# Attention with memory slots and a routed expert layer: queries loaded with the halves of a head's values on different partitions

## The chip, the cores and the metric

The kernel runs on one core of a Trainium2 chip. The core has a matrix engine (TensorE, "PE" in the profile), a vector engine (VectorE, "DVE"), an engine for activations (ScalarE, "ACT"), a general one (GpSimd, "POOL"), a sequencer that only issues transfers here (SyncE, "SP"), and 16 DMA engines. Data lie on 128 partitions in on-chip memory (SBUF); products of TensorE land in eight banks of PSUM. The metric is the time of one execution on the device in microseconds (us), as the median of several runs. Less is better.

## The reference

The first half is an attention with 32 memory slots, for 8 batches of 8 heads with 576 tokens of 64 values each. The second half routes each token (512 values, all its heads) to one of 8 experts, a two-layer network.

```python
a = softmax(phi)                       # over the 576 tokens, per slot
k_m = einsum('bhsm,bhsd->bhmd', a, k)  # 32 x 64 per head
v_m = einsum('bhsm,bhsd->bhmd', a, v)
scores = q @ k_m.T / 8                 # 576 x 32 per head
attn = softmax(scores)                 # over the 32 slots
x = attn @ v_m                         # 576 x 64 per head
logits = x @ w_gate + modality_bias[modality_id]
e = argmax(logits); gate = softmax(logits)[e]
out = gate * (relu(x @ w1[e]) @ w2[e])
```

Everything is float32.

## The kernel before, in words

The kernel finds out from the modality biases which expert the tokens will choose, loads that expert's two matrices once, and works on the assumption that all tokens go there; at the end it checks this, and would run a general path otherwise (it does not with these inputs).

**A batch has a memory step, a scores step and an expert step.** P = 128 partitions, HG = 4 heads (index j) by NG = 2 groups (index g) make the 8 heads. QP = 64 partitions hold a group's tokens, QC = 9 tokens on each. BL = 32 is the block that DVE's transpose turns by itself: a 32x32 block at a time, with no exchange between groups of 32 partitions. RA = 4 and RB = 5 columns of tokens make the two parts of a batch.

The memory step: the largest phi of each slot is found on DVE (`mem_max` and what follows), the exponentials are taken (`mem_exp`), their sums over a partition's nine tokens are made on POOL (`mem_sums`, lines 279 to 283). `kv_products` (line 388) multiplies them with keys and values on TensorE, in tiles of 64 rows by 32 columns, and then adds up the sums over partitions in eight small products (line 396). `kv_divide` divides: DVE makes the reciprocals (lines 472, 474), ACT scales (lines 482, 484). The keys are written twice each there, because the queries lie so that a head's 64 values are in two blocks of 32 on the *same* partitions, and need the keys of each half on every 32 partitions. `mem_turn` then turns keys and values with TensorE (line 146: two turns for the halves of the keys, one for the values), and ACT copies them from PSUM to SBUF (lines 514, 522).

The scores step: the queries, loaded by one DMA per batch (`load_queries`, line 180), are turned in place by DVE in four pieces, one for each j (`q_turn`, line 552). `scores` (line 564) multiplies them on TensorE with the keys in tiles of 32 rows by 32 columns: for each half u, each j, each g and each half a of a group's tokens one product, and the two halves u are added up in PSUM. `soften` and `normalise` make the softmax on DVE and ACT, and turn the weights so that slots lie on partitions (lines 591 to 623); `a_split` makes two parts of them, of which the expert products take one after the other (lines 657, 660).

The expert step: instead of multiplying the weights with the values and that with the first matrix, the kernel multiplies values and matrix first (`value_products`, line 730, in 64x32 tiles). `hidden` (line 776) then makes a piece of the hidden layer from the weights, ACT and DVE take the positive part in two parts (lines 789, 793), and `outputs` (line 812) multiplies with the second matrix. Each product of float32 values is made as three products of rounded parts. ACT scales a finished tile by the gate into one of two buffers `ob` (line 825), and SP stores it (lines 833, 837).

**What sets the order.** The instructions of each engine are written out in one order by a planner (`weave`): two lists, one of attention steps with due times and one of expert steps, are merged with the help of a table of durations (`TAKES`), rules for when a step's inputs are ready, and due times (`AHEAD`, `SPREAD`). No scheduler moves anything afterwards. Each engine goes through its list in order and waits where an input is not there yet. SP has one list as well: loads of keys, values, phi and queries, the stores of the outputs, and copies of the weights to DRAM. A DMA of SP waits for its buffer to be free, and all that stands behind it on SP waits too.

The queries of batch b + 2 are asked for right after the scores of batch b, whose buffer (`q_sb[b % 2]`) they take. Those of batch 1 come at the end of the first loads (`more_keys(0)`).

Of the kernel before, what the change touches and what calls it, by code (L numbers as in the profile page):

```python
# [54 lines left out]
def attn_moe(ctx: ExitStack, tc: tile.TileContext, q, k, v, phi, mod_id, w_gate, mod_bias, w1, w2, out):  # L55
# [23 lines left out]
    BUSY = 90, 10  # L79
# [23 lines left out]
    places = const.tile([P, 2], F32, name="places")  # L103
    busy = const.tile([P, 512], BF16, name="busy")
# [4 lines left out]
    kTs = [const.tile([P, 2, P], F32, name=f"kT{i}") for i in range(2)]  # L109
    vT = [const.tile([P, HG, M], F32, name=f"vT{b}") for b in range(B)]  # L110
# [31 lines left out]
    live = {}  # L142
# [35 lines left out]
    def load_queries(b, c0=0, n=QC):  # L178
        cols = slice(c0 * D, (c0 + n) * D)
        nc.sync.dma_start(q_sb[b % 2][:, :, cols], halves(q, b)[:, :, cols])  # L180
# [196 lines left out]
    def kv_products(b):  # L377
# [4 lines left out]
        live["psum"] = pk[:, :, 2 * D]  # L382
# [10 lines left out]
        for j in range(HG):  # L393
            for g in range(NG):
                half = slice(QP * g, QP * (g + 1))
                nc.tensor.matmul(
                    pk[M * j:M * (j + 1), g, 2 * D:2 * D + 1], lhsT=sums[half, j], rhs=ones_c[half],
                    start=True, stop=True, tile_position=(QP * g, M * j),
                )
# [30 lines left out]
    def first_divide():  # L430
# [11 lines left out]
        live["keys", 0] = wk.tile([P, 2, NG, 2, BL], F32, name="keys", bufs=2)  # L442
        live["values", 0] = wk.tile([P, NG, D], F32, name="values", bufs=2)
# [26 lines left out]
    def kv_divide(b):  # L470
# [5 lines left out]
        live["keys", b] = wk.tile([P, 2, NG, 2, BL], F32, name="keys", bufs=2)  # L476
        live["values", b] = wk.tile([P, NG, D], F32, name="values", bufs=2)
        for t in range(2):
            for g in range(NG):
                src = live["kvp"][:, g, t]  # L480
                if t:
                    nc.scalar.activation(live["values", b][:, g], src, AF.Copy, scale=rec[:, g])
                else:
                    nc.scalar.activation(
                        live["keys", b][:, :, g],
                        src.rearrange("p (u o d) -> p u o d", u=2, o=1).broadcast_to([P, 2, 2, BL]),
                        AF.Copy, scale=rec[:, g],
                    )
# [857 lines left out]
```

## Time and profile before

| what | before |
|---|---|
| median of 3 runs | 392.82 us (392.59 to 393.16) |
| the profiled execution | 392.55 us, its span 390.8 us |
| PE busy | 379.2 us, 97% of the span |
| DVE, ACT, POOL busy | 243.7, 144.8, 45.7 us |
| granted TensorE clock | 0.998 |
| scores, batches 1 to 7 (line 564, 32x288) | 448 records, 11.2 us of overlapping durations |
| key and value products (line 388) | 1008 records of 271 ns |
| sums (line 396) | 112 records of 167 ns |
| turns of keys and values (line 146), batches 1 to 7 | 14 and 7 records of about 272 ns |
| load of a batch's queries | 1152 KB, 7.8 us from issue to landing (median of 7) |
| DMA | 56.91 MB in 28700 packets |

The span runs from the first to the last instruction; the rest of an execution's time lies around it. A row of the chain or of a timeline has the start, the duration, the engine and the line, the tiles written and read, and how many instructions it stands for. Matmuls overlap: each has a duration of its own, and several run at once, so that what a group costs is read from starts and not from the sum of durations. A product of two float32 operands appears as two records. The mark [0.31 <-POOL sums] at a row's end says that the engine was idle that long before it and what ended the wait.

### The profile page before, as it was taken

How to read it: one execution, taken by the hardware profiler on the slowest of the kernel's cores; microseconds unless marked ns; L12 is line 12 of the kernel's file. 1: busy time of each engine (PE TensorE's matmuls, PEld its weight loads, DVE VectorE, ACT ScalarE, POOL GpSimd, SP SyncE). 2: the span in 40 equal slices, each digit the busy share in tenths (PEclk: the TensorE clock that was granted, in tenths of full speed). 3: DMA queues.
4: the chain of work that ended last, by engine and by line, in shares of the span. 5: the costliest groups of instructions: out<-in, count | busy, mean ns of one | idle time of the engine just before them, and what ended most of it. 6: DMA issues, size and time to landing. Idle time of an engine off the chain costs nothing.

```text
span 390.8 us, 10131 instructions
## 1 busy us (share of the span) xinstructions
PE 379.2 (97%) x4218; PEld 305.1 (78%) x4220; DVE 243.7 (62%) x613; ACT 144.8 (37%) x348; POOL 45.7 (12%) x112
## 2 busy tenths in 40 slices
PE   7899999999999999999999999999999999999993
PEld 3577885889679787887879887797868879698982
DVE  4787756895789377844786466864787558660400
ACT  2382434426234243433433334324432425250410
POOL 3247020023000300030000300003000200000000
PEclk9999999999999999999999999999999999999999
DMA  8999349435920672529111291514411011431112
GB/s 294 352 378 375 78 117 381 140 147 129 332 64 27 197 285 108 189 66 375 41 27 55 71 393 73 216 27 142 159 27 29 28 30 29 167 130 29 30 28 61
DMA packets 28700, 56.91 MB, mean 146 GB/s; under 512 B 3044, under 2 KB 8164, under 8 KB 28644
## 3 DMA queue, kind: packets, MB, share of 16 engines
q1 hardware_dynamic: 28368, 55.87, 42.6%
q8 instruction: 35, 0.57, 0.6%
q10 hardware_dynamic: 276, 0.30, 0.2%
q14 instruction: 21, 0.17, 0.1%
HBM read 37.28 MB, written 18.87 MB: 144 GB/s over the span
## 4 chain that ended last, share of the span: by engine, by line
PE 86%; DVE 5%; DMA 3%; ACT 2%; POOL 1%; issue 1%; SPq 0%; ACTq 0%; POOLq 0%
PE pe L812 48%; PE pe L776 26%; PE pe L730 3%; PE pair L564 3%; PE pair L388 3%; DMA q_sb<-in_q_dram 3%; PE pair L677 1%; PE pair L146 1%; DVE a L597 1%; ACT ob L825 1%; DVE a L591 0%; DVE mx L595 0%; PE pair L541 0%; POOL t2sums L279 0%; ACT exp L356 0%
## 5 line engine op out<-in xcount | busy, mean ns | idle before, releaser
L812 PE MATMUL pe<-w2h,hh 128*128 128x512 f32 x288 | 116.5, 405 | 0.0
L812 PE MATMUL pe<-w2h,hl 128*128 128x512 f32 x288 | 112.6, 391 | 0.0
L812 PE MATMUL pe<-w2l,hh 128*128 128x512 f32 x288 | 110.3, 391 | 0.0
L793 DVE SCALAR_TENSOR_TENSOR hl<-pe,hh 128x256 fp32r<-128x256 f32 (+2 forms) x158 | 57.9, 392 | 41.9 <-ACT hh L789 41.1
L812 PEld LDWEIGHTS pe<-w2h,hh 128*128 128x128 f32 x288 | 54.1, 188 | 21.2 <-issue 11.0
L789 ACT ACTIVATE hh<-pe 128x256 fp32r<-128x256 f32 (+2 forms) x158 | 53.3, 362 | 39.1 <-PE pe L776 38.7
L812 PEld LDWEIGHTS pe<-w2l,hh 128*128 128x128 f32 x288 | 54.0, 188 | 11.8
L812 PEld LDWEIGHTS pe<-w2h,hl 128*128 128x128 f32 x288 | 54.2, 188 | 9.6
L825 ACT ACTIVATE ob<-pe,gates 128x512 f32<-128x512 f32 x36 | 24.7, 689 | 77.5 <-issue 43.5
L776 PE MATMUL pe<-xbh,vwh 128*128 128x320 f32 x128 | 40.2, 314 | 0.1
L776 PE MATMUL pe<-xbh,vwl 128*128 128x320 f32 x128 | 39.5, 309 | 0.0
L776 PE MATMUL pe<-xbl,vwh 128*128 128x320 f32 x128 | 39.5, 309 | 0.0
L776 PE MATMUL pe<-xah,vwh 128*128 128x256 f32 x124 | 35.2, 286 | 0.6 <-ACT xah L657 0.4
L776 PE MATMUL pe<-xal,vwh 128*128 128x256 f32 x124 | 35.0, 284 | 0.3 <-DVE xal L660 0.3
L776 PE MATMUL pe<-xah,vwl 128*128 128x256 f32 x124 | 34.9, 283 | 0.0
L322 POOL COPY ts<-tm 32x4 f32<-32x4 f32 x24 | 4.8, 199 | 200.4 <-DVE tm L314 199.7
L776 PEld LDWEIGHTS pe<-xah,vwh 128*128 128x128 f32 x124 | 23.6, 191 | 3.1 <-ACT xah L646 1.6
L776 PEld LDWEIGHTS pe<-xbh,vwh 128*128 128x128 f32 x128 | 24.0, 188 | 1.2 <-issue 0.5
L776 PEld LDWEIGHTS pe<-xbl,vwh 128*128 128x128 f32 x128 | 24.0, 188 | 0.3
L776 PEld LDWEIGHTS pe<-xal,vwh 128*128 128x128 f32 x124 | 23.7, 191 | 0.8 <-DVE xal L660 0.5
L152 DVE TENSOR_TENSOR vwl<-pe,vwh 128x512 fp32r<-128x512 f32 x26 | 16.6, 678 | 12.0 <-ACT vwh L151 12.0
L776 PEld LDWEIGHTS pe<-xbh,vwl 128*128 128x128 f32 x128 | 24.0, 188 | 0.0
(171 smaller groups left out, 448.9 us busy)
## 6 DMA issues: line engine op xcount, KB each, us to landing
kv_sb<-in_k_dram SPq DMA_DIRECT2D x8, 1152.0 KB, 5.9
kv_sb<-in_v_dram SPq DMA_DIRECT2D x8, 1152.0 KB, 9.4
out_dram<-ob SPq DMA_DIRECT2D x64, 128.0 KB, 2.4
q_sb<-in_q_dram SPq DMA_DIRECT2D x7, 1152.0 KB, 7.8
ph<-in_phi_dram SPq DMA_DIRECT2D x7, 576.0 KB, 4.1
raw<-in_moe_w_dram SPq DMA_DIRECT2D x2, 1024.0 KB, 7.5
raw<-in_moe_w_dram SPq DMA_DIRECT2D x1, 1280.0 KB, 10.6
out_dram<-ob SPq DMA_DIRECT2D x4, 256.0 KB, 2.4
```

Of the source, the lines that this page charges most:

```text
L146: nc.tensor.transpose(dst, src, ident[:rows, :rows])
L152: nc.vector.tensor_tensor(l, src, h.bitcast(F32), op=ALU.subtract)
L322: nc.gpsimd.tensor_copy(ts_[BL * a:BL * (a + 1)], live["tm"][BL * o:BL * (o + 1)])
L388: nc.tensor.matmul(live["kvp"][M * j:M * (j + 1), g], lhsT=pe[half, j, c * M:(c + 1) * M], rhs=kv_sb[half, :, j, c * D:(c + 1) * D], start ...
L564: nc.tensor.matmul(sc[g][M * j:M * (j + 1), a, c0 * BL:(c0 + n) * BL].rearrange("p (c t) -> p c t", t=BL), lhsT=kTs[b % 2][p0:p0 + BL, u, ...
L597: nc.vector.tensor_tensor(x, x, m.broadcast_to(list(x.shape)), op=ALU.subtract)
L730: nc.tensor.matmul(pvs[g][M * j:M * (j + 1), :], lhsT=vT[b][rows, j, :], rhs=raw1[rows, j, cols], start=True, stop=not more, tile_position ...
L776: nc.tensor.matmul(ph[:, 0:n], lhsT=(vl if k == 2 else vh)[:, g, cols], rhs=xl if k == 1 else xh, start=(g == k == 0), stop=(g == NG - 1 a ...
L789: nc.scalar.activation(hs[0][:, f, h0:h0 + p1 - p0], live["ph", f][:, p0:p1], AF.Relu)
L793: nc.vector.scalar_tensor_tensor(hl, live["ph", f][:, p0:p1], 0.0, hh.bitcast(F32), op0=ALU.max, op1=ALU.subtract)
L812: nc.tensor.matmul(po, lhsT=tile_columns(hl if n == 1 else hh, f, t), rhs=(w2l if n == 2 else w2h)[:, f, :], start=(f == n == 0), stop=(f ...
L825: nc.scalar.activation(ob, po, AF.Copy, scale=gate_of(b, t))
```

## The change

From batch 1 on, queries are loaded in another layout. A token's 64 values are cut in halves u, and the halves go to different groups of 32 partitions: partition 64 g + 32 u + t holds, for each j, the half u of tokens 18 t to 18 t + 17. After DVE's turn (as before) the 64 values of a head lie on 64 partitions, and one token column is one moving column. So `scores` makes one product for each a, j and g, with 64 rows, and nothing is added up in PSUM. Batch 0 keeps the old layout (`first_scores`, `first_keys`).

- The load of a batch becomes 16 DMAs, one for each g, u and j, of 32 partitions with 18 runs of 128 bytes each. They are put in a list (`later`), and `load_some` issues one at each call of `hidden` or `outputs`. Batch 1's 16 are issued at once.
- Keys are not doubled any more: keys and values are divided together into one tile `kvn` (two ACT instructions instead of four), turned with two turns instead of three, and copied to `kvT` by one ACT copy instead of two.
- The sums over partitions are one product of 128 rows, 128 columns and two moving columns (`sides`, ones on the half of the partitions that belongs to g) instead of eight of one column.
- Since a group's tokens now lie as 2 t + a instead of 32 a + t, `normalise` writes the turned weights to every second column.
- The planner's table and rules get new numbers: `kv`, `kvT` and `s` shorter, the step after the sums at 1.2 instead of 1.8 before their end, batch 3's due times 4.0 later. Two more small products are made at the start to keep TensorE busy.

```diff
+    sides = const.tile([P, NG], F32, name="sides")
...
-    kTs = [const.tile([P, 2, P], F32, name=f"kT{i}") for i in range(2)]
-    vT = [const.tile([P, HG, M], F32, name=f"vT{b}") for b in range(B)]
+    kT0 = const.tile([P, 2, P], F32, name="kT0")
+    kvT = [const.tile([P, 1 + (b > 0), P], F32, name=f"kvT{b}") for b in range(B)]
+    vT = [x[:, int(b > 0)].rearrange("p (j m) -> p j m", j=HG) for b, x in enumerate(kvT)]
...
     def load_queries(b, c0=0, n=QC):
-        cols = slice(c0 * D, (c0 + n) * D)
-        nc.sync.dma_start(q_sb[b % 2][:, :, cols], halves(q, b)[:, :, cols])
+        if b == 0:
+            cols = slice(c0 * D, (c0 + n) * D)
+            nc.sync.dma_start(q_sb[b % 2][:, :, cols], halves(q, b)[:, :, cols])
+            return
+        src = q[b].rearrange("(j g) (t x) (u d) -> g u j t x d", g=NG, t=BL, u=2)
+        for g in range(NG):
+            for u in range(2):
+                p0 = QP * g + BL * u
+                to = q_sb[b % 2][p0:p0 + BL].rearrange("t j (x d) -> t j x d", d=BL)
+                for j in range(HG):
+                    later.append((to[:, j], src[g, u, j]))
+
+    def load_some(n=1):
+        for _ in range(min(n, len(later))):
+            nc.sync.dma_start(*later.pop(0))
...
-        for j in range(HG):
-            for g in range(NG):
-                half = slice(QP * g, QP * (g + 1))
-                nc.tensor.matmul(
-                    pk[M * j:M * (j + 1), g, 2 * D:2 * D + 1], lhsT=sums[half, j], rhs=ones_c[half],
-                    start=True, stop=True, tile_position=(QP * g, M * j),
-                )
+        nc.tensor.matmul(live["psum"], lhsT=sums.rearrange("p j m -> p (j m)"), rhs=sides, start=True, stop=True)
...
+        live["kv", b] = wk.tile([P, 2, NG, D], F32, name="kvn", bufs=2)
+        for g in range(NG):
+            nc.scalar.activation(live["kv", b][:, :, g], live["kvp"][:, g], AF.Copy, scale=rec[:, g])
...
             load_queries(1)
+            load_some(16)
...
+    def mem_turn(b):
+
+        to = pair_of_banks(1)[:, 0, 0:2 * P]
+        for t in range(2):
+            turn(to[:, t * P:(t + 1) * P], live["kv", b][:, t].rearrange("p g d -> p (g d)"))
+        nc.scalar.copy(kvT[b].rearrange("p t s -> p (t s)"), to)
...
+    def scores(b):
         sc = [pair_of_banks(g) for g in range(NG)]
+        qT = q_sb[b % 2].rearrange("p j (a x) -> p j a x", a=2)
+        for a in range(2):
+            for j in range(HG):
+                for g in range(NG):
+                    rows = slice(QP * g, QP * (g + 1))
+                    nc.tensor.matmul(
+                        sc[g][M * j:M * (j + 1), a, 0:QC * BL], lhsT=kvT[b][rows, 0, M * j:M * (j + 1)],
+                        rhs=qT[rows, j, a], start=True, stop=True, tile_position=(QP * g, M * j),
+                    )
...
-                nc.vector.transpose(aT[:, g].rearrange("p (c a t) -> p a c t", a=2, t=BL), a[:, g])
+                nc.vector.transpose(aT[:, g].rearrange("p (c t a) -> p a c t" if b else "p (c a t) -> p a c t", a=2, t=BL), a[:, g])
...
     def hidden(i, part, f, terms=range(3), groups=range(NG), to=None, evict=True):
 
 
+        load_some()
...
     def outputs(t, fs, finish, terms=range(3)):
 
 
+        load_some()
...
-    AHEAD, SPREAD = (5.8, 5.0), 0.55
+    AHEAD, EARLIER, SPREAD = (5.8, 5.0), {3: -4.0}, 0.55
...
-            t = max([0.0] + [done[n] + (0.1 if n[0] != "sums" else -1.8) for n in s[0][2] if n[0] != "g"])
+            t = max([0.0] + [done[n] + (0.1 if n[0] != "sums" else -1.2) for n in s[0][2] if n[0] != "g"])
```

The order of instructions at three places, before and then with the change. First PE from the sums of batch 1 to its scores (L388 key and value products, L396 sums, L812 expert products, L146 turns, L564 scores; with the change L403, L408, L816, L148, L548).

```order
L388 MATMUL pair_941<-kv_sb,exp 32x128 x72
L396 MATMUL pair_941<-ones_c,sums 32x1 x8
...
L812 MATMUL pe<-w2h,hh 128x512
L812 MATMUL pe<-w2h,hl 128x512
L812 MATMUL pe<-w2l,hh 128x512
L146 MATMUL pair_1051<-ident,keys 128x128 x2
L146 MATMUL pair_1051<-ident,values 128x128
L812 MATMUL pe<-w2h,hh 128x512
L812 MATMUL pe<-w2h,hl 128x512
L812 MATMUL pe<-w2l,hh 128x512
L564 MATMUL pair_1060<-q_sb_102,kT_79 32x288 x2
```

```order
L403 MATMUL pair_980<-kv_sb,exp 32x128 x72
L408 MATMUL pair_980<-sides,sums 128x2
...
L816 MATMUL pe<-w2h,hh 128x512
L816 MATMUL pe<-w2h,hl 128x512
L816 MATMUL pe<-w2l,hh 128x512
L148 MATMUL pair_1077<-ident,kvn 128x128 x2
L816 MATMUL pe<-w2h,hh 128x512
L816 MATMUL pe<-w2h,hl 128x512
L816 MATMUL pe<-w2l,hh 128x512
L548 MATMUL pair_1084<-q_sb_102,kvT_81 32x288
```

Nine expert products stood between sums and turns, now six; batch 2 alone keeps the twelve shorter ones that it had. The scores are 16 rows of one product each, where they were 16 rows of two.

Second, PE at batch 6: the key and value products inside the expert products of one output tile (pe_3602, with the change pe_3573; each group of three rows is one step of that tile).

```order
L812 MATMUL pe_3602<-w2h_107,hh_113 128x512
L812 MATMUL pe_3602<-w2h_107,hl_114 128x512
L812 MATMUL pe_3602<-w2l_108,hh_113 128x512
L388 MATMUL pair1_3615<-kv_sb_103,exp_3581 32x128 x72
L396 MATMUL pair1_3615<-ones_c_73,sums_3589 32x1 x8
L812 MATMUL pe_3602<-w2h_107,hh_113 128x512
```

```order
L816 MATMUL pe_3573<-w2h_107,hh_113 128x512
L816 MATMUL pe_3573<-w2h_107,hl_114 128x512
L816 MATMUL pe_3573<-w2l_108,hh_113 128x512
L403 MATMUL pair1_3589<-kv_sb_103,exp_3552 32x128 x72
L408 MATMUL pair1_3589<-sides_75,sums_3560 128x2
L816 MATMUL pe_3573<-w2h_107,hh_113 128x512
```

Before, four groups of three expert products of that tile come ahead of L388; now five do, so the products start three expert products later in the tile. Batch 2's stand where they stood.

Third, SP from the loads of batch 1's keys on (L176 keys and values, L180 queries, L837 output stores, L173 phi; with the change L178, L195, L841, L175).

```order
L176 DMA kv_sb<-in_k_dram 128x4x576
L176 DMA kv_sb<-in_v_dram 128x4x576
L180 DMA q_sb_102<-in_q_dram 128x4x576
L180 DMA q_sb_101<-in_q_dram 128x4x576
L837 DMA out_dram<-ob 64x512 x4
L173 DMA ph_104<-in_phi_dram 128x4x288
L173 DMA ph_105<-in_phi_dram 128x4x288
```

```order
L178 DMA kv_sb<-in_k_dram 128x4x576
L178 DMA kv_sb<-in_v_dram 128x4x576
L195 DMA q_sb_102<-in_q_dram 32x18x32 x16
L195 DMA q_sb_101<-in_q_dram 32x18x32 x16
L841 DMA out_dram<-ob 64x512 x4
L175 DMA ph_104<-in_phi_dram 128x4x288
L175 DMA ph_105<-in_phi_dram 128x4x288
```

Where one DMA stood for batch 1 and one for batch 2, 16 stand each, ahead of the first four output stores. Later batches' 16 are spread over the following stores and copies in groups of 2 to 13.

More of the change, by code (lines that the diff above doesn't have):

```diff
@@ L78, in attn_moe @@
     EPS = 1e-9
-    BUSY = 90, 10
+    BUSY = 92, 10
     FAR = float(1 << 20)
@@ L141, in attn_moe @@
     stage_pool = stage_ctx.enter_context(tc.tile_pool(name="stage", bufs=1, side="right"))
-    live = {}
+    live, later = {}, []
     def turn(dst, src, rows=P):
@@ L441, in first_divide @@
         live["recs"] = recs
-        live["keys", 0] = wk.tile([P, 2, NG, 2, BL], F32, name="keys", bufs=2)
-        live["values", 0] = wk.tile([P, NG, D], F32, name="values", bufs=2)
+        live["keys", 0] = wk.tile([P, 2, NG, 2, BL], F32, name="keys")
+        live["values", 0] = wk.tile([P, NG, D], F32, name="values")
         first_even(0)
@@ L474, in kv_divide @@
         nc.vector.reciprocal(rec[:, :, 0], den)
[L476 to L488, printed above, removed]
+        live["kv", b] = wk.tile([P, 2, NG, D], F32, name="kvn", bufs=2)
+        for g in range(NG):
+            nc.scalar.activation(live["kv", b][:, :, g], live["kvp"][:, g], AF.Copy, scale=rec[:, g])
     def more_keys(b):
@@ L505, in mem_kv, with first_keys @@
         more_keys(b)
[L507 to L532 removed]
+    def mem_turn(b):
[3 more added lines that the diff above has]
+        nc.scalar.copy(kvT[b].rearrange("p t s -> p (t s)"), to)
+    def first_keys():
+        to = pair_of_banks(0)[:, 0, 0:2 * P]
+        for u in range(2):
+            turn(to[:, u * P:(u + 1) * P], live["keys", 0][:, u].rearrange("p g o d -> p (g o d)"))
+        nc.scalar.copy(kT0.rearrange("p u s -> p (u s)"), to)
     def first_values():
[L535 to L536 removed]
+        to = bank("pe")[:, 0:P]
+        turn(to, live["values", 0].rearrange("p g d -> p (g d)"))
+        nc.scalar.copy(vT[0].rearrange("p j m -> p (j m)"), to)
     def mem_gate(b):
@@ L552, in q_turn, with first_scores @@
         nc.vector.transpose(x, x)
-    def scores(b, c0=0, n=QC):
+    def scores(b):
         sc = [pair_of_banks(g) for g in range(NG)]
-        qT = q_sb[b % 2].rearrange("p j (c u t) -> p j c u t", u=2, t=BL)
+        qT = q_sb[b % 2].rearrange("p j (a x) -> p j a x", a=2)
[7 more added lines that the diff above has]
+                    )
+        live["sc", b] = sc
+        if b + 2 < B:
+            load_queries(b + 2)
+    def first_scores(c0, n):
+        sc = [pair_of_banks(g) for g in range(NG)]
+        qT = q_sb[0].rearrange("p j (c u t) -> p j c u t", u=2, t=BL)
         cs = slice(c0, c0 + n)
@@ L954, in plan_first @@
         add(("vn", 0), "vn0", [("v", 0)], first_even, 1)
-        add(("s", 0, 0), "s0", [("kT", 0), ("qt", 0, 0, 1)], scores, 0, 0, RA)
+        add(("s", 0, 0), "s0", [("kT", 0), ("qt", 0, 0, 1)], first_scores, 0, RA)
         add(("vo", 0), "ko0", [("vn", 0)], first_odd, 1)
@@ L995, in plan_first @@
         turns(1, 1, 27.2)
-        add(("s", 0, 1), "s1", [("qt", 0, 1, 1), ("vwl", 0, 1)], scores, 0, RA, RB, floor=28.6)
+        add(("s", 0, 1), "s1", [("qt", 0, 1, 1), ("vwl", 0, 1)], first_scores, RA, RB, floor=28.6)
     def plan_steps(b, dues):
@@ L1213, in attn_moe @@
         nc.scalar.activation(minus, ident, AF.Copy, scale=-1.0)
+        for g in range(NG):
+            for e in range(NG):
+                nc.gpsimd.memset(sides[QP * g:QP * (g + 1), e:e + 1], float(g == e))
         for j in range(HG):
```

33 lines of the change are left out of this document (6 added, 27 removed), and 6 rows, old and new, of the table TAKES.

## The prediction

> **What bounds the kernel now.** I read the page first (busy time, slices, the chain of waits), then the chain piece by piece over one batch, then the engines' timelines at the places that the change touches.
>
> ```profile
> PE 379.2 (97%) x4218; PEld 305.1 (78%) x4220; DVE 243.7 (62%) x613; ACT 144.8 (37%) x348; POOL 45.7 (12%) x112
> PE   7899999999999999999999999999999999999993
> PE 86%; DVE 5%; DMA 3%; ACT 2%; POOL 1%; issue 1%; SPq 0%; ACTq 0%; POOLq 0%
> ```
>
> PE is busy in nine tenths or more of every slice but the first two and the last, and 86% of the chain is PE. So time is saved only by taking work off PE or closing one of its few gaps; what DVE, ACT or POOL save is worth nothing by itself. One batch of the chain (start, duration, what; the first row is from the start of the kernel, the last a pair of value products for comparison):
>
> ```profile
> 2.28 11.52 DMA q_sb<-in_q_dram
> ...
> 129.49 2.08 PE pair L388 x138
> 131.70 2.30 PE pe L812 x9
> 134.00 0.33 PE pair L146 x3
> 134.32 1.40 PE pe L812 x6
> 135.72 1.53 PE pair L564 x63
> ...
> 150.35 1.02 PE pe L730 x16
> ```
>
> The memory step of a batch stands inside the expert products: key and value products (L388) with their sums (L396), nine expert products (L812), three turns (L146), six more, the scores (L564). An expert product costs 1.40/6 = 0.233. The timeline of PE has the piece at the sums:
>
> ```profile
> 129.41 2.25 PE L388 MATMUL pair<-kv_sb,exp 64*32 64x128 f32 x144
> 131.40 0.29 PE L396 MATMUL pair<-ones_c,sums 64*32 64x1 f32 x16
> 131.63 0.50 PE L812 MATMUL pe<-w2h,hh 128*128 128x512 f32 x1
> 131.97 0.40 PE L812 MATMUL pe<-w2h,hl 128*128 128x512 f32 x1
> ```
>
> A float32 product has two records, so 72 key and value products are 144. They pass in 131.40 - 129.41 = 1.99. The first expert product behind them takes 131.97 - 131.63 = 0.34 instead of 0.233: going back from small tiles to the whole array costs 0.1.
>
> **Scores: 32 products of 32 rows become 16 of 64 rows,** all with 288 columns, in batches 1 to 7. Count columns passed, divided by the tiles that the array holds: 32 x 288 / 16 = 576 before and 16 x 288 / 8 = 576 after. Before, this takes 1.53, or 2.66 ns per column. The two rows with 64x32 tiles are cheaper: L388 has 72 x 128 / 8 = 1152 columns in 1.99 (1.73 ns), L730 has 8 products of 512 columns on 8 tiles, 512 in 1.02 (1.99 ns). So the new scores lie between 576 x 1.73 = 0.99 and 576 x 1.99 = 1.15; the other end is no gain, 1.53. I take 1.15, because L730 is nearest in length (one round of long products, start and end included). Saved: 0.38 x 7 = 2.66.
>
> **Turns: three become two.** 0.33/3 = 0.11 each; 0.11 x 7 = 0.77 saved. The two ACT copies behind them become one, and four ACT divisions become two; both are off PE's path (ACT 37% busy).
>
> **Sums: eight products of one column on 64x32 tiles become one 128x128 product of two columns.** Before, 131.63 - 131.40 = 0.23 up to the next product. Afterwards two records, each of which needs the whole array's weights: nearest is the turn, 0.11 a record, so 0.22, plus the 0.1 for going back to the whole array, which now falls ahead of the sums and no longer behind them: 0.32. Bounds: 0.13 (no more than one turn's worth beyond today's drain) to 0.50. I take 0.32, a loss of 0.09 x 7 = 0.63.
>
> **Six expert products instead of nine between sums and turns** (all batches but batch 2, as the order shows). What runs meanwhile, by the timelines of DVE and ACT:
>
> ```profile
> 131.88 0.16 DVE L472 TENSOR_SCALAR den<-pair 128x2 f32<-128x2 f32 x1 [4.89 <-PE pair L396]
> 132.07 0.17 DVE L474 RECIPROCAL rec<-den 128x2 f32<-128x2 f32 x1
> 132.33 0.62 ACT L484 ACTIVATE keys<-pair,rec 128x128 f32<-128x128 f32 x2 [4.59 <-DVE rec L474]
> 132.84 0.52 ACT L482 ACTIVATE values<-pair,rec 128x64 f32<-128x64 f32 x2
> ```
>
> Two activations of 128 columns stay, so the turns' input is there at 132.33 + 0.62 = 132.95, about 1.3 after the sums end (131.69). Six products last 0.34 + 5 x 0.233 = 1.5 from 131.63, to 133.13. That is a margin of 0.2: I charge 0. If the cover is gone (the sums 0.5 long, or ACT held by an output), up to 0.3 in six batches.
>
> **PE's gaps.** Two kinds lie near the change:
>
> ```profile
> 266.63 2.25 PE L388 MATMUL pair<-kv_sb,exp 64*32 64x128 f32 x144
> 269.19 0.27 PE L396 MATMUL pair<-ones_c,sums 64*32 64x1 f32 x16 [0.31 <-POOL sums L283]
> ...
> 68.33 0.38 PE L776 MATMUL pe<-xah,vwh 128*128 128x256 f32 x1 [0.39 <-ACT xah L657]
> 69.06 0.39 PE L776 MATMUL pe<-xal,vwh 128*128 128x256 f32 x1 [0.34 <-DVE xal L660]
> ```
>
> In batch 6 the sums start 269.19 - 266.63 = 2.56 after the products instead of 1.99: PE loses 0.57 to POOL. In the new order these products stand three expert products (0.70) later, so the 0.57 goes. The gap of batch 1 (0.39 + 0.34) hangs on the chain from scores to weights; scores and use both move earlier, so it stays.
>
> **Strided turns of the weights.** L623 now writes every second column. No row has such a store; bounds are nothing and a doubling of
>
> ```profile
> L623 DVE STREAM_TRANSPOSE aT<-a 128x256 f32<-128x256 f32 x14 | 5.4, 421 | 0.1
> L591 DVE STREAM_TRANSPOSE a<-pair 128x256 f32<-128x256 f32 x16 | 6.3, 430 | 14.6 <-PE pair L564 14.6
> ```
>
> where blocks scattered 64 columns apart (L623) cost no more than gathered ones (L591). So I take a tenth, 0.1, once: only batch 1 waits for it (the gap above); at worst 2 x 0.42 = 0.84.
>
> **Query loads: one of 512 runs of 2304 bytes becomes 16 with 9216 runs of 128 bytes per batch.** SP's rows, the landings, and windows (fourth column from the end of a window row on: clock, share of DMA, GB/s):
>
> ```profile
> 9.71 0.76 SPq L227 DMA_DIRECT2D mid<-in_moe_modality_id_dram  x1
> 10.51 0.61 SPq L231 DMA_DIRECT2D wg<-in_moe_w_gate_dram  x1
> 23.46 9.11 SPq L180 DMA_DIRECT2D q_sb<-in_q_dram  x2
> 44.11 2.45 SPq L837 DMA_DIRECT2D out_dram<-ob  x4
> ...
> mid<-in_moe_modality_id_dram SPq DMA_DIRECT2D x1, 36.0 KB, 7.4
> wg<-in_moe_w_gate_dram SPq DMA_DIRECT2D x1, 16.0 KB, 6.8
> ...
> 14.00:16.00 2.00, 0.95 (x22) 0.54 (x14) 1.89 (x6) 0.31 (x2) 0.00 (x0) 1.00 1.15 271
> 18.00:20.00 2.00, 2.00 (x33) 0.47 (x17) 1.86 (x7) 1.42 (x3) 1.77 (x8) 1.00 1.05 389
> 38.00:40.00 2.00, 2.00 (x10) 1.52 (x9) 1.71 (x3) 0.17 (x1) 0.00 (x0) 1.00 0.49 181
> 93.00:138.00 45.00, 44.87 (x674) 35.37 (x657) 30.74 (x76) 15.82 (x40) 4.54 (x11) 1.00 0.47 152
> ...
> 52.05 2.09 DVE L552 STREAM_TRANSPOSE q_sb<-q_sb 128x576 f32<-128x576 f32 x3
> 58.57 0.70 ACT L825 ACTIVATE ob<-pe,gates 128x512 f32<-128x512 f32 x1
> ```
>
> The loads of mid and wg are 512 runs each of 72 and 32 bytes. They landed by 9.71 + 7.4 = 17.1 and 10.51 + 6.8 = 17.3, and the window at 14 moved 271 GB/s where one full of long runs moved 389: 236 KB less, 0.61 us of all 16 engines, over 1024 runs 0.61 x 16 / 1024 = 9.5 ns a run. A new load is then 576 runs x 9.5 ns = 5.5 beside its bytes (1152 KB at 389 GB/s = 3.0): 8.5 instead of 3.0. In a steady batch DMA is 47% busy over 45 us, so 5.5 fits, and a load has about a batch until its turn. Tightest is the start: DMA is full until about 39, of which the second q load is the last 3, so batch 1's queries start at about 33 and land at 42 instead of 36; DVE turns them at 52.05. The load behind it lands at 50 and holds the first output stores (ready at 44.11) on SP until then; the next ob is written at 58.57, its buffer needed only there. SP issues 16 loads at 0.61 to 0.76, 10 to 12 of 45. I cost it at 0.
>
> The Trainium skill, "DMA: Bandwidth & Descriptors", section "Why small descriptors are slow (HBM only)", says that each run carries a fixed part beside its bytes; it also asks for 512 bytes in "Specifications". By its three beats of overhead on the four of 128 bytes a load would be an estimated 3.0 x 7/4 = 5.3; the trace's row is dearer, and the sum would be the same by both.
>
> **Start.** Four small fills on POOL (places, below, has eight in 0.61) come ahead of a wait for mid of 1.55, and two more warm products ahead of the first queries' DMA in the chain: 0.
>
> ```profile
> 1.88 0.61 POOL L1216 MEMSET places<- 32x1 f32 x8
> 4.64 0.18 POOL L1222 CAST mid_f<-mid 1x1 f32<-1x1 int32 x1 [1.55 <-DMA mid<-in_moe_modality_id_dram]
> ```
>
> **Sum.** -2.66 - 0.77 + 0.63 - 0.57 + 0.10 = -3.27. The profiled execution took 392.55 (span 390.8 and 1.75 around it), so 389.28; the median of the runs shown, 392.82, is 0.27 above it, so I forecast **389.5**. Gains at the good ends (scores 0.99, sums 0.13, no strided cost): -3.78 - 0.77 - 0.70 - 0.57 = -5.82, or 387.0; at the bad ends (sums 0.50, strided 0.84): -2.66 - 0.77 + 1.89 + 0.84 - 0.57 = -1.27, or 391.5.
>
> **Rivals.** First, the scores gain nothing: the array's fill is the same 576 columns either way, and what makes them 2.66 ns a column (the start of two long rounds, the operands) stays. Then 389.5 + 2.66 = 392.2, no change. For it: equal fill. Against it: both rows of 64x32 tiles are at 1.73 to 1.99. The Trainium skill, "TensorEngine Tiling (Array Packing)", section "Available Configurations", lists 16 tiles of 32x32 and 8 of 64x32, the same cells; by that rule alone this rival holds, and the trace's 2.66 against 1.73 disagrees with it.
>
> Second, on the other side, **the queries come late**. One mechanism: a run of 128 bytes costs an engine far more than 9.5 ns, and the loads are served in turn. Batch 1's queries have from 33 to 52.05 for 576 runs an engine, so it decides from 33 ns a run. At 60 ns a load takes 34.6 and lands at 67.6; DVE's four turns (2.8) end at 70.4, and the scores, which PE now starts at about 60, wait 10; the next load ends near 102, when batch 2's scores are due, and costs 1 to 2 more: 389.5 + 11.5 = 401. Against it: the rate read above; for it, only that this rate is from 32 and 72 bytes beside long runs, in one window.
>
> Third, half of the gain is given back by waits in the memory step: sums at 0.50 and turns waiting 0.3 in six batches, at worst (0.50 - 0.32) x 7 = 1.26 and 0.3 x 6 = 1.8 on top of the sum; about half of the two, 1.5, would make it 391.0, still faster.
>
> **Chances.** Forecast 0.72, no gain in scores 0.10, late queries 0.10, half given back 0.08. A measurement of this kernel tells about 0.2%, 0.8 us, from no change. The forecast's own range, 387.6 to 391.5, lies below 392.0: faster 0.79; same 0.11 (the first rival and a little of the third); slower 0.10. The range to hold it 8 in 10 is 387.6 to 392.3: it takes in the first and third rivals and leaves out the second.
>
> **What would show it.** Right: score groups of 32 records passing in 1.0 to 1.2 from their start to the next product; two turns; sums in about 0.3; no PE gap ahead of turns or sums; q turns on DVE without a wait for DMA. Wrong: a DVE wait for q_sb near 52, an output that waits for a store, or scores still near 1.5.

## The result

| | median, us | runs |
|---|---|---|
| before | 392.99 | 4 (392.59 to 393.16) |
| changed | 389.69 | 4 (389.51 to 389.74) |

The ratio is 0.992, with a 95% interval of 0.9906 to 0.9933: the changed kernel is 3.3 us faster, against a forecast of 389.5. The number was right. The way to it was not: about 1 us of the 3.3 comes from where the loads' destinations lie in SBUF, a thing that the prediction did not look at, and stalls in batches 1 and 3 gave about as much back. That the two cancelled, and the sum came within 0.2 us of the time, is luck.

### The profile page after: what moved, and what is told of

Read it like the earlier page. It is cut to its first block, busy times and chain, and to the rows that moved or that the text cites. A ratio compares the mean times of both kernels' runs of the same rounds, so it can differ in the third digit from the quotient of the medians.

```text
span 387.9 us, 9645 instructions
## 1 busy us (share of the span) xinstructions
PE 375.3 (97%) x3891; PEld 303.3 (78%) x3893; DVE 244.7 (63%) x613; ACT 141.3 (36%) x327; POOL 45.8 (12%) x116
## 4 chain that ended last, share of the span: by engine, by line
PE 85%; DVE 4%; SPq 4%; DMA 3%; ACT 1%; issue 1%; ACTq 0%
PE pe L816 47%; PE pe L779 24%; PE pair L403 4%; PE pe L732 3%; DMA q_sb<-in_q_dram 3%; SPq L195 3%; PE pair L548 2%; PE pair L679 1%; SPq L178 1%; DVE vwl L154 1%; PE pair L148 1%; PE pair L732 1%; PE pair L408 1%; DVE xbl L662 0%; ACT ob L829 0%
## 5 line engine op out<-in xcount | busy, mean ns | idle before, releaser
L816 PE MATMUL pe<-w2h,hh 128*128 128x512 f32 x288 | 116.3, 404 | 0.0
L816 PE MATMUL pe<-w2h,hl 128*128 128x512 f32 x288 | 112.4, 390 | 0.0
L816 PE MATMUL pe<-w2l,hh 128*128 128x512 f32 x288 | 110.3, 391 | 0.0
L796 DVE SCALAR_TENSOR_TENSOR hl<-pe,hh 128x256 fp32r<-128x256 f32 (+2 forms) x158 | 58.3, 392 | 43.1 <-ACT hh L792 42.3
L816 PEld LDWEIGHTS pe<-w2h,hh 128*128 128x128 f32 x288 | 54.1, 188 | 19.8 <-issue 9.7
L816 PEld LDWEIGHTS pe<-w2l,hh 128*128 128x128 f32 x288 | 54.0, 188 | 11.8
L816 PEld LDWEIGHTS pe<-w2h,hl 128*128 128x128 f32 x288 | 54.2, 188 | 9.6
L779 PEld LDWEIGHTS pe<-xah,vwh 128*128 128x128 f32 x124 | 23.6, 191 | 4.2 <-ACT xah L648 1.6
L779 PEld LDWEIGHTS pe<-xah,vwl 128*128 128x128 f32 x124 | 23.7, 191 | 0.0
```

The lines of the kernel that those rows point to most:

```text
L779: nc.tensor.matmul(ph[:, 0:n], lhsT=(vl if k == 2 else vh)[:, g, cols], rhs=xl if k == 1 else xh, start=(g == k == 0), stop=(g == NG - 1 a ...
L796: nc.vector.scalar_tensor_tensor(hl, live["ph", f][:, p0:p1], 0.0, hh.bitcast(F32), op0=ALU.max, op1=ALU.subtract)
L816: nc.tensor.matmul(po, lhsT=tile_columns(hl if n == 1 else hh, f, t), rhs=(w2l if n == 2 else w2h)[:, f, :], start=(f == n == 0), stop=(f ...
```

## The profile after

The page of the changed kernel, first PE's busy time and slices, then the chain's shares:

```profile
PE 375.3 (97%) x3891; PEld 303.3 (78%) x3893; DVE 244.7 (63%) x613; ACT 141.3 (36%) x327; POOL 45.8 (12%) x116
PE   6899999999999999999999999999999999999993
PE 85%; DVE 4%; SPq 4%; DMA 3%; ACT 1%; issue 1%; ACTq 0%
```

PE bounds the kernel as before. SP's queue is new in the chain, with 4%: it is the issuing of batch 1's query loads, from 22.4 to 35.6 us, and the chain goes from there over a landing at 38.20 to a turn of the weights on DVE. DVE is not idle before that turn (its row of two turns starts at 37.79, right behind the instruction ahead), so this share is no lost time. The chain piece by piece (start, duration, what): the first queries' load, then the memory and scores step that the prediction showed from 129.49 on.

```profile
2.29 10.43 DMA q_sb<-in_q_dram
...
131.91 2.18 PE pair L403 x144
134.08 0.31 PE pair L408 x2
134.40 1.50 PE pe L816 x6
135.90 0.22 PE pair L148 x2
...
138.58 1.13 PE pair L548 x32
```

Scores take 1.13 instead of 1.53, the turns 0.22 instead of 0.33, and there are six expert products in 1.50 ahead of them. The piece from the first key product to the turns is 135.90 - 131.91 = 3.99; before it was 134.00 - 129.49 = 4.51 with three products (0.70) more, so the wide sums cost 3.99 + 0.70 - 4.51 = 0.18. The first load takes 10.43 instead of 11.52.

The gain was followed through the program by the start of the first hidden product of each batch, which is the same work in each kernel. The third column is a kernel of the experiments below: the kernel before with its tiles 32 bytes further on.

| first hidden product of batch | before | before, moved | changed | changed - before | changed - moved |
|---|---|---|---|---|---|
| 0 | 21.57 | 20.68 | 20.49 | -1.08 | -0.19 |
| 1 | 68.33 | 67.48 | 67.65 | -0.68 | +0.17 |
| 2 | 118.78 | 118.12 | 117.13 | -1.65 | -0.99 |
| 3 | 161.55 | 160.93 | 159.28 | -2.27 | -1.65 |
| 4 | 209.83 | 209.23 | 208.15 | -1.68 | -1.08 |
| 5 | 252.60 | 252.03 | 250.58 | -2.02 | -1.45 |
| 6 | 301.35 | 300.81 | 298.47 | -2.88 | -2.34 |
| 7 | 344.12 | 343.61 | 340.90 | -3.22 | -2.71 |

Four things stand in the table that the sum of the prediction did not have. 1.08 us are there before any product of the changed steps has run. Batch 1 loses 0.4. Between batches 3 and 4 about 0.6 net is given back. And batch 2 gains more than its share: before, its key and value products took 2.62 in PE's timeline instead of 2.25, beside a 16-KB fetch of instructions (91.8 to 93.2); in the changed kernel they take 2.25. The longer time stands in all three profiles of the old program (2.40 to 2.66 from the first of these products to the first sum, where another batch has 1.99).

**Batch 3's loss** is on DVE. Its timeline, and PE's (the last bracket is the idle time ahead and what ended it):

```profile
160.88 0.68 DVE L294 TENSOR_TENSOR t2top<-ph 128x512 f32<-128x512 f32 x1
162.38 0.29 DVE L298 TENSOR_TENSOR top<-top,ph 128x128 f32<-128x128 f32 x1
162.59 1.41 DVE L796 SCALAR_TENSOR_TENSOR hl<-pe,hh 128x256 fp32r<-128x256 f32 x4
...
163.06 0.39 PE L779 MATMUL pe<-xah,vwh 128*128 128x256 f32 x1 [0.74 <-DVE hl L796]
```

The next batch's maxima (L294 to L298) stand ahead of the remainders of the hidden layer (L796). The ring of four PSUM banks is full until a remainder frees one, and PE waits 0.74. The changed order put batch 3's memory step four microseconds later. In experiment 4, which takes this back, the same maxima stand at the same place ahead of the remainders, but end 0.7 earlier (161.97 instead of 162.67). There the gate's products (L679) come ahead of the second group of value products (L732); here they come behind them, and DVE is idle for 1.74, to 156.51, until ACT has copied the values (vwh).

**Batch 1's loss** is in the memory and scores step, in the chain of the changed kernel:

```profile
58.11 0.43 PE pair L148 x2
58.53 0.70 PE pe L816 x3
59.24 1.50 PE pair L548 x30
```

ACT's copy of the turned keys, and all waits at the score line:

```profile
58.57 0.37 ACT L512 COPY kvT<-pair 128x256 f32<-128x256 f32 x1
...
L548 PEldq EVENT_SEMAPHORE  x42: 51/51/51, 58.1 to 314.4; - x42
```

Here the turns take 0.43 and the scores 1.50, nothing of the gain of a later batch. Only three expert products stand between them. The copy of the turned keys stands behind an output on ACT (58.57 to 58.94), and the score products of this kernel wait for 16 separate loads: the trace has 42 waits of their own at L548 where the kernel before had 14 at its line. In batch 1 seven of them follow the copy, one per 0.125 us from 59.0 to 59.7, in the time of the products themselves.

## The experiments

Each ratio is to runs of the kernel before on the same chip.

### 1. The kernel before, again

No edit; it asks whether the load's 11.52 is chance.

> The kernel before, unchanged, for a second profile of its start. In the first pair of profiles the changed kernel's first queries landed 1.09 us earlier (12.72 against 13.80), ahead of anything that the change touches but two more warm products and four small fills. If that is chance from one execution to the next, this start lies elsewhere than at 13.8 by some tenths or more, and the whole follows it; if the change makes it, the first queries land at 13.8 again. Time 392.8 either way, within 0.3%.

392.73 us (ratio 0.9997, 0.9985 to 1.0009), and its load took 11.47:

```profile
2.28 11.47 DMA q_sb<-in_q_dram
```

So the 1.09 at the start belongs to the change.

### 2. Each score product cut in two

```diff
-    nc.tensor.matmul(sc[g][..., a, 0:QC * BL], ..., rhs=qT[rows, j, a], ...)
+    for cs in (slice(0, QC * BL // 2), slice(QC * BL // 2, QC * BL)):
+        nc.tensor.matmul(sc[g][..., a, cs], ..., rhs=qT[rows, j, a, cs], ...)
```

> The changed kernel with each of the 16 score products cut into two of 144 columns: 32 products, 64 records, in the same tiles over the same columns. If the old scores were slow because of the number of records (in the trace of before, the first 32 records start in bursts and the rest one each 16.7 ns), a score group goes back from 1.13 to about 1.5, 0.35 x 7 = 2.5 more: 392.2. If they were slow because of the 32x32 tiles, a group stays at 1.13 to 1.2 and the time at 389.7 to 390.2.

392.96 us (ratio 1.0, 0.9987 to 1.0013), 3.3 more than the changed kernel. The chain has

```profile
179.62 1.51 PE pair L549 x58
```

for the same 576 columns on the same eight tiles of 64x32. With 64 records instead of 32, the group is back at the 1.53 of before. The columns passed, divided by the tiles, are 576 in all three kernels (1.53, 1.13, 1.51), so the gain is not that of the tile shape by itself: it goes when the products are halved in length and doubled in number. Going by the chains, 32 records more cost about 0.4 us, 12 ns each.

A fixed price for a record is not shown by this. The key and value products pass 144 records on the same 64x32 tiles in 1.99 before the change, 13.8 ns each, where the old scores took 23.9 (1.53 / 64) and the cut ones 23.6 (1.51 / 64). Each record of the scores also has a load of weights of its own (224 of both at L548), so it may be these that set the pace. Why the groups differ stays open.

The time rose by more than the 2.5 of the theory: the seven groups are 2.7 longer together, counted from their first product to the next other one, and batch 2's key and value products take 2.54 up to the sums instead of 2.18, beside a fetch of instructions at 92.0, as in the kernel before.

### 3. Eight small products for the sums, as before

```diff
-    live["psum"] = pk[:, 0, 2 * D:2 * D + NG]
+    live["psum"] = pk[:, :, 2 * D]
...
-    nc.tensor.matmul(live["psum"], lhsT=sums..., rhs=sides, start=True, stop=True)
+    for j in range(HG):
+        for g in range(NG):
+            half = slice(QP * g, QP * (g + 1))
+            nc.tensor.matmul(pk[M * j:M * (j + 1), g, 2 * D:2 * D + 1], lhsT=sums[half, j], rhs=ones_c[half], ...)
```

> The changed kernel with the sums over partitions as before: eight products of one column on 64x32 tiles. In the trace of the changed kernel, products and sums take 2.42 from the first key product to the next expert product where they took 2.22 before, and the going back to the whole array costs nearly the same. If the one wide product is dearer by its two loads of weights, this is 0.15 to 0.2 faster a batch, 1.05 to 1.4 in all: 388.4. If its cost is only that of going back to the whole array, which the small ones pay behind them, no change: 389.7.

390.85 us (ratio 0.9956, 0.9935 to 0.9977): slower than the changed kernel by 1.2, against the expectation. Most batches did gain 0.17 in the trace. But in batch 4 PE stands still in the middle of the sums:

```profile
171.89 2.25 PE L403 MATMUL pair<-kv_sb,exp 64*32 64x128 f32 x144
173.88 0.23 PE L411 MATMUL pair<-ones_c,sums 64*32 64x1 f32 x9
175.68 0.24 PE L411 MATMUL pair<-ones_c,sums 64*32 64x1 f32 x7 [1.54 <-issue]
```

It waits for nothing that the profile shows ("issue"); from 173.1 to 174.3 the trace has a 16-KB fetch of instructions, and there is another stop of 0.26 in batch 2, about 1 us behind the end of the fetch of 92.1. That the instructions came late is inferred from this coincidence; no run moved a fetch. Against it, the kernel before has a fetch at 173.95 beside its eight sums of batch 4 (174.22), and no stop there. The wide product costs 0.18 a batch, and the changed kernel has none of these stops.

### 4. Batch 3's memory step at its old place

```diff
-    AHEAD, EARLIER, SPREAD = (5.8, 5.0), {3: -4.0}, 0.55
+    AHEAD, EARLIER, SPREAD = (5.8, 5.0), {}, 0.55
```

> The changed kernel without the 4.0 that put batch 3's due times later; its key products come 15 expert products earlier, about where they stood before. In the changed kernel PE stops 0.74 at 162.3 for DVE, which is late with the hidden layer because value weights, gate and the next batch's maxima stand ahead of it. If the shift of batch 3 causes that, the stop goes and the time falls by about 0.9 to 388.8. If the stop comes from the shorter batch itself, it stays or moves and the time stays at 389.7.

389.37 us (ratio 0.9905, 0.9876 to 0.9934). The wait of 0.74 is gone and the trace is 0.70 ahead behind it; 0.2 is given back later, where there is a new wait of the turns for POOL:

```profile
PE pair L148 <- POOL vg L256: 0.6, 1, 0.6
```

The intervals of this kernel and the changed one overlap, so the 0.3 between them isn't shown by the times; that the later step causes the wait for hl is.

### 5 and 6. Where the tiles lie

The changed kernel has a new small tile ahead of the large ones, and other tiles changed size. By the addresses of the two programs the query tiles start 480 bytes past a multiple of 512 before, and at a multiple of 512 after, and so do the tiles behind them for keys, values, phi and the raw first-layer weights. (The raw second-layer weights lie elsewhere and did not move.) Each kernel was given the other's place by an unused tile:

```diff
+    pad = const.tile([P, 8], F32, name="pad")      # the kernel before: 32 bytes
     busy = const.tile([P, 512], BF16, name="busy")
```

```diff
+    pad = const.tile([P, 120], F32, name="pad")    # the changed kernel: 480 bytes
     busy = const.tile([P, 512], BF16, name="busy")
```

> The kernel before with one unused tile of 32 bytes a partition put ahead of the warm-up tile, nothing else. It moves every large tile of SBUF up by 32 bytes: the query, key and raw-weight tiles, which started 480 bytes past a multiple of 512 bytes, start at a multiple of 512, as they do in the changed kernel (there because of its new tile for the sums). Theory (the start's gain of 1.09 us in the changed kernel is the place of the load's destination, not an edit of the work): the first queries' load takes about 10.5 us instead of 11.5, their packets of 2304 bytes about 94 ns instead of 97, and the kernel 391.7 us (391.3 to 392.0). Rival (the gain comes from the two more warm-up products or from the fills on GpSimd): no change, 392.8.

> The changed kernel with an unused tile of 480 bytes a partition at the same place, so that the large tiles start 480 bytes past a multiple of 512 again, as before the change. Theory (place of the destination): the first queries' load takes 11.5 us again and the kernel 390.7 us (390.4 to 391.0), which is what the change to the work alone is worth: about 2.1 us less than before. Rival (warm-up products or fills): 389.7.

391.78 us (ratio 0.9979, 0.997 to 0.9988) and 390.94 us (ratio 0.9952, 0.9933 to 0.9971): both times are as the theory of the place had them. The load is so in the first pair alone: 10.63 instead of 11.52. In the second it went from 10.43 to 10.96 only, and not back to 11.5. The rows are the load in the chain and the window from 10 to 12 us (its last number is GB/s), in the kernel before:

```profile
10.00:12.00 2.00, 1.93 (x69) 1.61 (x60) 1.47 (x4) 0.26 (x2) 0.00 (x0) 1.00 1.08 364
```

in the same moved by 32 bytes:

```profile
10.00:12.00 2.00, 1.94 (x72) 1.68 (x64) 1.37 (x6) 0.00 (x0) 0.00 (x0) 1.00 1.07 391
...
2.27 10.63 DMA q_sb<-in_q_dram
```

and in the changed kernel moved by 480:

```profile
10.00:12.00 2.00, 1.95 (x75) 1.70 (x70) 1.44 (x4) 0.24 (x2) 0.00 (x0) 1.00 1.08 364
...
2.29 10.96 DMA q_sb<-in_q_dram
```

With DMA equally busy (1.07 to 1.08), 7% more bytes pass in this window when the tiles start at the multiple. The start moves by 0.89 in the first pair (table above) and by 0.53 in the second. So between 0.53 and 0.89 of the 1.08 are the place of the tiles. With the tiles at the multiple the old program's load (10.63) lies within those of the changed one's kernels (10.31 to 10.63); off it, 11.47 and 11.52 stand against 10.96 and 10.99, and where that half microsecond comes from was not found.

One window is short: the other kernels of this study with tiles at the multiple moved 373 to 397 GB/s in it. The load's own packets are the steadier measure. They carry 1024 bytes each (512 of them; the packets of 2304 bytes are keys and values), and took 46.0 ns on average in all nine profiles with the query tiles at a multiple of 512, and 49.6 to 49.7 in the three at 480 past it.

The profile of the moved changed kernel loses another 0.93 in batch 1, and this is the rival of the late queries in another form. Its chain and ACT's timeline there:

```profile
55.08 4.27 DMA out_dram<-ob
...
60.46 1.74 PE pair L549 x30
...
59.45 0.69 ACT L830 ACTIVATE ob<-pe,gates 128x512 f32<-128x512 f32 x1 [0.87 <-DMA out_dram<-ob]
60.04 0.36 ACT L513 COPY kvT<-pair 128x256 f32<-128x256 f32 x1
```

The first output stores stand on SP behind the query loads. In the changed kernel as it is, SP's timeline reads

```profile
27.19 25.25 SPq L195 DMA_DIRECT2D q_sb<-in_q_dram  x30
52.56 2.87 SPq L841 DMA_DIRECT2D out_dram<-ob  x4
```

so 30 loads hold SP at 0.84 each (most take 0.63; the first of them longer), and the stores that were issued at 44.11 before go out at 52.56. The buffer is wanted at 57.93. Two microseconds more on SP (54.48 in the moved kernel), and the output waits 0.87 for its store, the copy of the keys waits behind the output, and PE behind the copy.

### 7 and 8. How coarse the boundary is

```diff
+    pad = const.tile([P, 16], F32, name="pad")     # 64 bytes; in the other kernel P, 64: 256 bytes
     busy = const.tile([P, 512], BF16, name="busy")
```

> The changed kernel with an unused tile of 64 bytes a partition, so that its large tiles start 64 bytes past a multiple of 512. It tells how coarse the boundary is that a load's destination has to keep. If 32 or 64 bytes are enough: no change, 389.7 us and 10.4 us for the first queries' load. If it is 128 bytes or more: as with 480 bytes, 390.9 us (390.5 to 391.2) and 11.0 us or more for that load.

> The same with 256 bytes: the large tiles start 256 bytes past a multiple of 512. If the boundary is 256 bytes or finer: no change, 389.7 us. If it is 512: 390.9 us (390.5 to 391.2).

| tiles start past a multiple of 512 by | median, us | ratio to before | first load, us | GB/s, 10 to 12 us |
|---|---|---|---|---|
| 0 (changed) | 389.69 | 0.992 (0.9906 to 0.9933) | 10.43 | 390 |
| 64 | 390.87 | 0.9947 (0.9929 to 0.9964) | 10.99 | 366 |
| 256 | 389.91 | 0.9927 (0.991 to 0.9943) | 10.38 | 394 |
| 480 | 390.94 | 0.9952 (0.9933 to 0.9971) | 10.96 | 364 |

A start at a multiple of 256 bytes is as good as one of 512; 64 past it is as bad as 480 (224 past). The packets of the first load say the same: 46.0 ns at 256, 49.7 at 64. (In the profile of the 64-byte kernel the granted clock fell to 0.50 from 18 to 20 us, behind the landing of this load at 13.28, so only its load and its window are compared.) Whether 128 would do wasn't tried. The Trainium skill, "DMA: Bandwidth & Descriptors", section "How a descriptor splits into AXI transactions", states a boundary of 256 bytes for what a descriptor reads: where one starts off it, the bytes from the boundary below are fetched too and cost beats. The runs agree with the 256 and show it at the destination in SBUF. They do not agree with the section's counting of beats: for a run of 1024 bytes (32 beats) that would be an estimated two more beats at 64 and seven at 224, while the two measured the same (49.7 and 49.6 ns).

### 9. Batch 1's scores three products later

Without the later step of batch 3, as in experiment 4, and:

```diff
-    if b == 0 and t == 3 and f == 1:
+    if b == 0 and t == 3 and f == 2:
         next_values(0)
...
-    "kvT": (0.45, "A0.4"),
+    "kvT": (0.45, "A0.4"), "kvT1": (0.45, "A1.0"),   # kvT1: batch 1's
```

> The changed kernel without the four microseconds by which batch 3's memory step was put later (as in the run without them, 389.4 us), and with three expert products more between batch 1's turn and its scores: six in place of three; nothing else moves. Theory (batch 1 lost 0.4 us because the scores' waits, one for each of 16 loads, and the copy of the turned keys come too late behind only three products): batch 1's group of score products goes from 1.50 to about 1.13 us, the 0.37 us wait for the copy goes, and the time is 389.0 us (388.8 to 389.2). Rival (the stop moves on to the next step: the softened weights come 0.7 us later and the products that need them wait as much longer): 389.4 to 389.8.

390.43 us (ratio 0.9949, 0.993 to 0.9968): the rival, and more than it said. The chain shows why:

```profile
58.57 1.38 PE pe L816 x6
59.95 1.13 PE pair L548 x32
...
66.70 1.05 ACT vwh L741 x2
67.75 0.53 ACT xah L659
```

The scores took 1.13, so the waits and the copy had cost batch 1 its 0.37, as the theory said. But DVE began with the scores 0.40 later than in experiment 4 (61.25 instead of 60.85), and ACT now takes the value copies (vwh) ahead of the softened weights (xah), which brings these to 67.64 instead of 66.93, 0.71 later. From batch 1 on the trace is 0.5 to 0.7 behind experiment 4's. In batch 1 the end is set by the chain from the scores over DVE and ACT, not by PE's work.

### 10. The old rule for what follows the sums on POOL

```diff
-    t = max([0.0] + [done[n] + (0.1 if n[0] != "sums" else -1.2) ...])
+    t = max([0.0] + [done[n] + (0.1 if n[0] != "sums" else -1.8) ...])
```

> The changed kernel with the order's old rule for what follows the sums on GpSimd (1.8 us ahead of their end instead of 1.2), so the memory products are put earlier again. Theory (the wait for GpSimd of before comes back where the products stand ahead of the sums' end): one or more waits of PE for GpSimd of 0.3 to 0.6 us a batch, 390.2 us (389.9 to 391.2). Rival (since there is one product of the sums now, and it stands behind the 72 key and value products, it waits for nothing): 389.7.

389.95 us (ratio 0.9933, 0.9915 to 0.9951), 0.26 over the changed kernel and not told apart from it by the intervals. PE's waits have the row again

```profile
PE pair L408 <- POOL sums L298: 0.5, 2, 0.3
```

one of 0.31 in batch 6, where the kernel before lost its 0.57, and one of 0.24 in batch 3. The trace falls back by 0.38 around the first. A lead of 0.3 that this kernel had from batch 1 on goes around the second. So the rule is worth about 0.4 in batch 6 and 0.3 in batch 3.

### 11. Every query load issued twice

```diff
         later.append((to[:, j], src[g, u, j]))
+        later.append((to[:, j], src[g, u, j]))
...
-        load_some(16)
+        load_some(32)
```

> The changed kernel with every load of queries from the second batch on issued twice (32 loads a batch instead of 16, the same bytes to the same places), which doubles the runs of 128 bytes. Theory (the loads end long before the turn of the queries needs them, at 13 ns a run): within 0.4 us of the changed kernel, 389.5 to 390.1, and the turns of queries wait for no transfer. Rival of the prediction (late queries): a batch's load takes twice as long and the scores wait, 2 us or more a batch where it is already near, over 395 in all.

603.54 us (ratio 1.5354, 1.5294 to 1.5413), which neither theory had. What SP waited for:

```profile
SPq L196 <- DMA q_sb<-in_q_dram: 269.1, 112, 9.3
```

The second copy of a load writes where the first does, and the program makes it wait on SP until the first has landed: 112 waits, 269.1 us, and every store stands behind them. It tested a blocked queue and not the price of runs of 128 bytes. That price is read from the changed kernel's trace: its 64512 packets of 128 bytes took 13.0 ns each on average. DVE's turns of the queries waited

```profile
L539 DVE STREAM_TRANSPOSE q_sb<-q_sb 128x576 f32<-128x576 f32 (+2 forms) x32 | 22.6, 750 | 0.3 <-DMA q_sb<-in_q_dram 0.3
```

0.3 us in all, at the start, for batch 0's own first load. By how many runs more the queries would be late was not found.

### 12. The changes that helped, together

Experiment 4's kernel, and three unused tiles that bring the other transferred tiles (raw second-layer weights, the softened weights' second half, the outputs) to multiples of 512 bytes.

```diff
+    stage_pool.tile([P, 120], F32, name="pad")   # behind raw2; the same behind xb in its pool
+    wk.tile([P, 80], F32, name="pad")            # ahead of the outputs
```

> The changed kernel without the later memory step of batch 3 (389.4 us by itself), and with three unused tiles of 320 to 480 bytes a partition that put the other tiles that transfers write or read at multiples of 512 bytes: the raw second-layer weights, the second half of the softened weights and the output tiles, which start 480 and 192 bytes past one now. Theory (a transfer is slower when its tile in SBUF starts off such a boundary): the start gains again, if these transfers are on its path, 0.1 to 0.5 us: 389.1 us (388.8 to 389.4). Rival (only the first queries' load sets the start): 389.4.

389.22 us (ratio 0.991, 0.9891 to 0.9928), the lowest median of the study, but its interval overlaps the changed kernel's and experiment 4's. The start did not move. It is not shown to beat the changed kernel.

## Why the prediction was right, and where it was not

- **Scores, -2.66.** Right in size: 1.13 instead of the forecast 1.15 in six batches (1.11 in batch 2, by its starts), nothing in batch 1 (1.50), so about -2.4. The reason given, that columns are cheaper on 64x32 tiles, fell with experiment 2: on the same tiles the same columns took 1.51 in twice the records. The row at 1.99 ns a column (L730) has few records to its columns, 16 to 512; the row at 1.73 (L388) has 144 to 1152, more than the old scores with their 64 to 576, and was cheap all the same. So the rows that carried the forecast were not cheap for one reason, and that 1.15 came out is in part luck. The rival of no gain fell too. The rule that it leaned on (the Trainium skill, "TensorEngine Tiling (Array Packing)", section "Available Configurations": 16 tiles of 32x32 or 8 of 64x32) is true of the fill, and the fill was not what bound.
- **Turns, -0.77.** Right in six batches, where 0.33 became 0.22; in batch 1 they take 0.43, so about -0.56 in all.
- **Sums, +0.63.** The product itself took 0.31, forecast 0.32. But the comparison was with 0.23 of before, of which part was hidden; the piece as a whole is 0.18 longer, not 0.09: about +1.3 in seven batches. Undoing it brought 0.17 in most batches and stops of up to 1.54 elsewhere.
- **Six products instead of nine, 0.** Right: 1.50, and no gap ahead of the turns outside batch 1.
- **POOL's wait, -0.57.** Right; experiment 10 brings two thirds of it back in that batch.
- **Strided turns, +0.10.** They cost nothing: 0.80 for two of the strided, 0.77 for two of the other.
- **Query loads, 0.** From batch 1 on the turns never waited. A packet of 128 bytes took 13.0 ns with its bytes, so the 576 of an engine take 7.5 us; the forecast's 9.5 ns came on top of the bytes and made 8.5 us. Batch 1's packets moved from 31.0 to 42.6, with DMA 73% busy from 31 to 43 and SP issuing one load every 0.68 or so; that they end near 42, as forecast, fits the queue's pace rather than the price of a run. But the margin was not at the queries: it was at the stores behind them on SP, which the prediction saw and took for covered until 58.57. They were issued at 52.56, forecast about 50, and in the moved kernel they were too late by 0.87.
- **The start, 0.** The term that failed. It was -1.08, of which 0.53 (by the changed kernel moved) to 0.89 (by the kernel before moved) come from the address of the loads' destinations; the rest stays open. The prediction weighed the four fills and the two warm products and did not ask what a new tile does to the tiles allocated behind it.
- **No term at all** stood for batch 3's later memory step (a wait of 0.74), for batch 1's scores behind 16 waits (0.37), or for batch 2's key products, which had been 0.4 too long before, beside a fetch of instructions.

What the work of the change is worth, with the place the same, is therefore 389.69 - 391.78 = -2.09 at a multiple of 512 bytes (-2.3 by the ratios 0.992 and 0.9979, each to its own measurement of before) and 390.94 - 392.73 = -1.79 at 480 past it, not -3.27; by the table's last column the profiled executions have -2.71 + 0.19 = -2.52 from batch 0 to batch 7. The terms for a steady batch, -0.40, came out at -0.37 (batches 4 to 5 and 6 to 7 of that column). The forecast of 389.5 was hit because the start's gain and the losses of batches 1 and 3 were missed together. Of the work's 3.27, about 1.0 to 1.2 was given back (at the multiple), most of the 1.5 that the third rival put at 0.08, though not by the waits that it named.

## What to carry to other kernels

When a group of small products costs more than its columns, try fewer and longer products, and test the reason by cutting them again on the same tiles: here that gave the whole gain back. Before a time is put down to an edit, compare the addresses of all tiles that transfers write: the changed small tiles moved most loads' destinations by 32 bytes modulo 512, which was worth about a third of this change, and a pad in the kernel before is the control that shows it. When one transfer becomes many, cost the queue that issues them, with what stands behind it, and the waits that each consumer gets, and not only the bytes.

## What the runs showed of the hardware

- A load of 512 KB from HBM whose SBUF tile starts 64 or 224 bytes past a multiple of 256 took 10.96 to 11.52 us, 49.6 to 49.7 ns for a packet of 1024 bytes (four profiles). With the tile at a multiple of 256 it took 10.31 to 10.63 us, 46.0 ns a packet (ten profiles).
- 16 products of 64 rows in 32 records took 1.13 us; the same columns in 64 records, whether as 32-row tiles (1.53) or as half as many columns each (1.51), took 0.4 more.
- A product that reads a tile filled by many loads waits for each load apart; where no earlier work lets the waits run ahead they took 0.125 us each on PE.
- PE stopped for 1.54 us with no wait in the profile in a burst of small products, at the time of a 16-KB instruction fetch; another such fetch beside the same products, in the kernel before, stopped nothing.
- Transfers of 128-byte runs cost 13.0 ns a run and engine here, and SP about 0.63 us for each of 16 loads of 72 KB.
